# The last two output tiles of an attention-plus-MLP kernel: another copy out of PSUM and another cut of the store

## The chip, the cores and the metric

One core of one Trainium2 chip. The metric is device time of the whole program in microseconds, as the median of several executions of the compiled kernel; lower is better.

## What is computed

Attention with a position bias, batch 4, 8 heads, 576 positions, head dimension 64, and behind it a two-layer MLP with a squared ReLU on the 4 x 576 = 2304 token rows of 512 numbers. All inputs and the output are float32.

```python
def _attn_ref(q, k, v, w1, b1, w2):
    ...
    attn = np.exp(scores)
    attn = attn / (np.sum(attn, axis=-1, keepdims=True) + 1e-09)
    return np.matmul(attn, v).astype(np.float32)

def _moe_ref(x, w_in, w_out):
    h = x @ w_in
    r = np.maximum(h, 0.0)
    g = r * r
    return (g @ w_out).astype(np.float32)
```

`x` is the attention's output as a matrix of 2304 x 512, `w_in` is 512 x 2048, `w_out` 2048 x 512. Rows 576 b to 576 b + 575 of the result belong to batch b.

## The kernel before, in words

The program runs in two stages. The attention stage fills the first half of the span; the MLP stage is a hand-written order of work (`tc.manual_schedule()`, so the order of the code is the order on each engine). The change lies at the very end of the MLP stage.

The MLP stage walks over `items`, pairs of a token group `n` and a slice `P` of the hidden width. Groups 0 to 3 are the first 512 positions of each batch. The fifth group, `n == B`, holds the rest: the last 64 positions of each of the four batches, 256 rows in all, packed as two tiles of 128 rows. Tile k = 0 has the tails of batches 0 and 1, tile k = 1 those of batches 2 and 3, 64 partitions for each batch. This group comes last, and its last item is the last of the program.

For an item, `products` (line 1192) makes the hidden activations on TensorE, `sums`, `squares` and `parts_g` turn them into the operands `gh` and `gl` of the second layer, and `down` (line 1284) adds their products with `w_out` into PSUM banks `y`, one bank of 128 x 512 for each tile of 128 rows. For the very last item `down` sorts its matmuls by tile, so that tile 0 is complete before the matmuls of tile 1 begin. After the last matmul of a tile `down` calls `leave`, which copies the bank from PSUM into a fresh SBUF tile `o` and sends it to DRAM.

For groups 0 to 3 the store is line 1267: 512 KB, two tiles at a time, 128 partitions outermost. For the group of tails `leave` takes another path (lines 1246 to 1251): VectorE copies the right half of the bank (line 1247), ScalarE the left half (line 1248), and SyncE issues one transfer of 256 KB (line 1250). Its DRAM side is a view of `out` with the batch outermost: 2 batches x 64 rows x 512.

All transfers of the kernel before are issued by SyncE, on its one queue. ScalarE issues none. At the end (line 1403) SyncE waits for the transfers that are still under way, and then the engines meet and the program ends.

Of the kernel before, what the change touches and what calls it, by code (L numbers as in the profile page):

```python
# [21 lines left out]
B, H, S, D = 4, 8, 576, 64  # L22
# [55 lines left out]
def attention_then_relu2_mlp(ctx: ExitStack, tc: tile.TileContext, q, k, v, cols, w_in, w_out, psi, xmat, dist, out):  # L78
    nc = tc.nc
    PE, DVE, ACT, POOL, SP = nc.tensor, nc.vector, nc.scalar, nc.gpsimd, nc.sync  # L80
# [1151 lines left out]
    def pair_tile():  # L1232
        return stage_p["p"].tile([128, 2, 512], F32, name="o", tag="stage", bufs=2)
# [8 lines left out]
    def leave(n, P, k):  # L1242
        y = y_t[n][k]
        j, x = divmod(k, 2)
        if n == B:
            o = ready_y[j] = pair_tile()
            DVE.tensor_copy(out=o[:, 0, 256:], in_=y[:, 256:])
            ACT.copy(o[:, 0, :256], y[:, :256])
            tails = out.rearrange("(b s) m -> b s m", s=S)[2 * k:2 * k + 2, 512:]
            SP.dma_start(out=tails, in_=o[:, 0])  # L1250
            return
        if (n, 0) in part_y:
            o = ready_y[j]
            DVE.tensor_tensor(out=o[:, x], in0=o[:, x], in1=y, op=ALU.add)
        else:
            if x == 0:
                ready_y[j] = pair_tile()
            o = ready_y[j]
            ACT.copy(o[:, x], y)
        if x == 0:  # L1260
            return
        if P < NP - 1:
            ready_y[j, "dram"] = dram.tile([128, 1024], F32, name=f"py{j}")
            SP.dma_start(out=ready_y[j, "dram"], in_=o.rearrange("p x m -> p (x m)"))
        else:
            rows = out[S * n + 256 * j:S * n + 256 * j + 256].rearrange("(x p) m -> p x m", x=2)
            SP.dma_start(out=rows, in_=o)

    def down(i):
        n, P = items[i]  # L1270
        w = width[n]
        nk = w // 64
        if (n, P) in firsts:
            banks = {k: py_p.tile([128, 512], F32, name=f"y{k}") for k in (2, 3, 0, 1) if k < nk}
            y_t[n] = [banks[k] for k in range(nk)]
        order = [(f, k, m) for f in range(2) for ms in ((0, 1), (2,)) for k in range(nk) for m in ms]
        if i == NI - 1:
            order.sort(key=lambda x: x[1])
        for f, k, m in order:
            wh, wl = w_t[4 * P + 2 + f]  # L1280
            gh, gl = g_t[i, f]
            t, o = divmod(128 * k, w)
            slot = t if f else 1 - t
            PE.matmul(  # L1284
                y_t[n][k], lhsT=(gl if m == 2 else gh)[:, slot, o:o + 128], rhs=wl if m == 1 else wh,
                start=((n, P) in firsts and f == 0 and m == 0), stop=((n, P) in lasts and f == 1 and m == 2),
            )
            if (n, P) in lasts and f == 1 and m == 2:
                leave(n, P, k)
        if (n, P) in lasts and P < NP - 1:  # L1290
            for j in range(2):
                part_y[n, j] = ready_y[j, "dram"]

    tmp_p = tmp_stack.enter_context(tc.tile_pool(name="tmp", bufs=1, side="right", reuse_waits="tile"))
    with tc.manual_schedule():
# [3 lines left out]
        for i in range(NI + 1):  # L1299
# [49 lines left out]
            if i < NI and (n, P) in firsts:  # L1349
                r = run_of[n, P]  # L1350
# [56 lines left out]
```

## Time and profile before

| What | Value |
|---|---|
| Time, median of 3 runs | 713.63 us (713.4 to 714.18) |
| Span of the profiled execution, first to last instruction | 712.7 us |
| Own time of the profiled execution | not listed beside the span; the median of the runs is 0.93 us above the span |
| TensorE busy | 685.8 us, 96% of the span |
| VectorE busy | 552.1 us, 77% |
| ScalarE busy | 472.8 us, 66% |
| GpSimd busy | 196.7 us, 28% |
| DMA, mean over the span | 105 GB/s |

The profile is of one execution on the one core. Busy time is a mean over the whole span; the last stretch has to be read by itself, in views limited to a window of time. In those, SPq stands for an instruction of SyncE that issues a transfer: its duration is that of the issue, not of the transfer. The share of the DMA is the mean busy share of the core's 16 DMA engines, and packets are what these engines moved: one per row of 2 KB here, and a small one with which each participating engine reports that it is done.

### The profile page before, as it was taken

The numbers are of one execution on the slowest core, as the hardware profiler recorded it, in microseconds if no ns is written. First come the engines' busy times: TensorE is split into PE (matmuls) and PEld (weight loads), VectorE is DVE, ScalarE is ACT, GpSimd is POOL, SyncE is SP. The second block draws the span as 40 slices with busy tenths as digits, with TensorE's granted clock in tenths as the row PEclk, the third lists the DMA queues.
The fourth block names the chain that finished last, engine by engine and source line by source line (L and its number), as shares of the span: only waits on it lengthen the run. The fifth ranks groups of instructions, "written<-read, shape, count | busy, mean of one in ns | idle before, by whom it ended". The sixth has DMA issues, their size and how long they took to land.

```text
span 712.7 us, 17402 instructions
## 1 busy us (share of the span) xinstructions
PE 685.8 (96%) x6966; PEld 568.7 (80%) x6966; DVE 552.1 (77%) x1165; ACT 472.8 (66%) x954; POOL 196.7 (28%) x313
## 2 busy tenths in 40 slices
PE   7899999999999999999999999999999999999992
PEld 6678888887787877778788888888888888888881
DVE  7999888876688998998888868687567964566761
ACT  5678878878777999997666757765475554464220
POOL 5464544442111344653223113121111220000000
PEclk9999999999999999999999999999999999999997
DMA  6740000007476234111901433230076403433100
GB/s 190 209 118 3 19 2 3 2 19 219 171 246 205 55 94 128 65 31 56 359 1 61 184 127 119 86 136 1 1 246 256 149 22 142 176 105 119 60 2 29
DMA packets 31620, 75.13 MB, mean 105 GB/s; under 512 B 5556, under 2 KB 13876, under 8 KB 30516
## 3 DMA queue, kind: packets, MB, share of 16 engines
q1 hardware_dynamic: 31540, 74.03, 31.1%
q8 instruction: 55, 0.90, 0.5%
q14 instruction: 25, 0.20, 0.1%
HBM read 55.66 MB, written 18.35 MB: 104 GB/s over the span
## 4 chain that ended last, share of the span: by engine, by line
PE 86%; DVE 7%; ACT 2%; issue 1%; POOL 1%; DMA 0%; SPq 0%; ACTq 0%; POOLq 0%; DVEq 0%
PE y L1284 28%; PE ha L1192 13%; PE sp L425 11%; PE px L547 10%; PE hb L1192 9%; PE pp L529 8%; PE bb L383 5%; DVE t L438 2%; DVE mask L373 1%; ACT pt L1123 1%; PE pa L521 1%; ACT p L445 1%; DVE bt L391 1%; DMA area<-in_psi 0%; DVE xT L496 0%
## 5 line engine op out<-in xcount | busy, mean ns | idle before, releaser
L1192 PEld LDWEIGHTS <-area 128*128 128x128 f16 x1680 | 147.7, 98 | 25.3 <-issue 8.4
L1284 PE MATMUL y<-w,gh 128*128 128x512 f32 x576 | 149.0, 398 | 0.6 <-ACT gh L1228 0.6
L1284 PEld LDWEIGHTS y<-w,gh 128*128 128x128 f32 x576 | 105.1, 188 | 22.2 <-ACT gh L1228 1.3
L438 DVE CUSTOM_DVE_ANT_0 t<-sp,area 128x576 f32<-128x576 f32 x144 | 104.2, 753 | 22.4 <-PE sp L425 12.0
L445 ACT ACTIVATE p<-t,negm 128x576 f32<-128x576 f32 x144 | 113.0, 795 | 2.7 <-DVE negm L438 2.1
L425 PE MATMUL sp<-k,q 64*128 64x288 f32 (+1 forms) x640 | 98.9, 426 | 5.5 <-DVE negm L438 4.0
L547 PE MATMUL px<-pt,v 128*64 128x128 f32 (+1 forms) x1600 | 92.2, 266 | 0.0
L547 PEld LDWEIGHTS px<-pt,v 128*64 128x64 f32 x1600 | 79.2, 137 | 11.5 <-ACT pt L1123 6.4
L1192 PE MATMUL ha<-area 128*128 128x256 f16 (+1 forms) x816 | 85.1, 260 | 0.7 <-DVE c L1209 0.7
L399 POOL TENSOR_TENSOR area<-bt,bt 128x256 f32<-128x256 f32 x72 | 66.0, 921 | 69.1 <-DVE bt L391 67.5
L1284 PE MATMUL y<-w,gl 128*128 128x512 f32 x288 | 79.0, 390 | 0.0
L529 PE MATMUL pp<-ident,p 128*128 128x128 f32 x576 | 78.1, 278 | 0.0
L529 PEld LDWEIGHTS pp<-ident,p 128*128 128x128 f32 x576 | 62.6, 141 | 17.7 <-ACT p L445 7.2
L425 PEld LDWEIGHTS sp<-k,q 64*128 64x128 f32 (+1 forms) x640 | 52.9, 175 | 25.4 <-issue 6.1
L1192 PE MATMUL hb<-area 128*128 128x256 f16 (+1 forms) x612 | 64.7, 260 | 0.0
L1284 PEld LDWEIGHTS y<-w,gl 128*128 128x128 f32 x288 | 54.1, 188 | 12.2 <-DVE gl L1229 0.2
L373 DVE TENSOR_TENSOR mask<-sdist,theta 128x1024 f16<-128x1024 f16 x81 | 57.9, 720 | 2.5 <-PE bb L383 0.5
L851 ACT COPY pt<-pp 128x512 f32<-128x512 f32 x68 | 36.9, 589 | 32.2 <-PE pp L529 32.2
L383 PE MATMUL bb<-wmov,mask 128*128 128x64 f16 x1296 | 46.9, 197 | 4.2 <-DVE mask L373 4.1
L1123 ACT COPY pt<-pp 128x512 f32<-128x512 f32 x76 | 41.4, 602 | 13.5 <-PE pp L529 13.1
L383 PEld LDWEIGHTS <-mask 128*128 128x128 f16 x1296 | 44.9, 101 | 6.5 <-DVE mask L373 5.9
L1229 DVE TENSOR_TENSOR gl<-area,gh 128x512 fp32r<-128x512 f32 (+1 forms) x40 | 25.3, 668 | 27.3 <-ACT gh L1228 25.5
(161 smaller groups left out, 992.8 us busy)
## 6 DMA issues: line engine op xcount, KB each, us to landing
raw<-in_w_in SPq DMA_DIRECT2D x32, 512.0 KB, 4.4
r<-in_w_out SPq DMA_DIRECT2D x16, 512.0 KB, 5.3
xs<-area SPq DMA_DIRECT2D x4, 1792.0 KB, 12.7
py<-o SPq DMA_DIRECT2D x12, 512.0 KB, 2.7
o<-py SPq DMA_DIRECT2D x12, 512.0 KB, 4.5
v<-in_v SPq DMA_DIRECT2D x16, 320.0 KB, 3.9
q<-in_q SPq DMA_DIRECT2D x32, 128.0 KB, 3.5
out<-o SPq DMA_DIRECT2D x8, 512.0 KB, 2.9
```

What stands on the lines that cost most here:

```text
L373: DVE.tensor_tensor(out=out, in0=win, in1=th, op=ALU.is_ge)
L383: PE.matmul(bb[:, 64 * (7 - r):64 * (8 - r)], lhsT=m[:, r], rhs=wmov[:, n], start=(n == 0), stop=(n == 1))
L399: POOL.tensor_tensor(out=dst, in0=tw, in1=sw, op=ALU.add)
L425: mm = PE.matmul(out_t[to, x, :HALF], lhsT=qt[rows, cols], rhs=kt[rows, k0:k0 + HALF], start=True, stop=True)
L438: DVE.tensor_tensor_reduce(out=t.rearrange("p (x n) -> p x n", x=2), in0=sp[:, :, :HALF], in1=bias.rearrange("p (x n) -> p x n", x=2), sca ...
L445: ACT.activation(out=p[:, S * n:S * n + S], in_=t, func=AF.Exp, bias=negm[:, n:n + 1], scale=-1.0, accum_out=sums[:, 2 * ic + n:2 * ic + n ...
L529: PE.transpose(pp[:, 128 * c:128 * c + 128], p[:, k0:k0 + 128], ident)
L547: PE.matmul(px[64 * h:64 * h + 64, 128 * m:128 * m + w], lhsT=vt[:, c, h], rhs=src, start=(c == 0), stop=(c == 4))
L851: ACT.copy(dst, src)
L1123: ACT.copy(*c)
L1192: PE.matmul(h[:, s, :w], lhsT=a, rhs=x, start=(k == 0), stop=(k == 5))
L1284: PE.matmul(y_t[n][k], lhsT=(gl if m == 2 else gh)[:, slot, o:o + 128], rhs=wl if m == 1 else wh, start=((n, P) in firsts and f == 0 and m ...
```

## The change

The last two tiles leave PSUM in one VectorE copy each, 128 x 512, and ScalarE copies nothing there. Each tile then goes to DRAM as two transfers, one for each batch: 64 partitions of `o` to 64 consecutive rows of `out`, 128 KB, so that the rows are the outermost dimension on both sides. SyncE issues the first of the two, ScalarE the second.

```diff
         if n == B:
             o = ready_y[j] = pair_tile()
-            DVE.tensor_copy(out=o[:, 0, 256:], in_=y[:, 256:])
-            ACT.copy(o[:, 0, :256], y[:, :256])
-            tails = out.rearrange("(b s) m -> b s m", s=S)[2 * k:2 * k + 2, 512:]
-            SP.dma_start(out=tails, in_=o[:, 0])
+            DVE.tensor_copy(out=o[:, 0], in_=y)
+            for r, queue in enumerate((SP, ACT)):
+                end = S * (2 * k + r + 1)
+                queue.dma_start(out=out[end - 64:end], in_=o[64 * r:64 * r + 64, 0])
             return
```

On ScalarE the end of the program changes as follows (`gh` are the operands of the last matmuls, `y_9466` and `y_9467` the PSUM banks of tiles 0 and 1):

```order
 L1206 ACTIVATE area<-ha,small 128x4x128
 L1228 CAST gh<-area 128x2x128 x2
-L1248 COPY o<-y_9466 128x256
-L1248 COPY o<-y_9467 128x256
+L1250 DMA out<-o 64x512 x2
 L1403 UNCONDITIONAL_BRANCH
```

The two copies are gone and two issues of transfers stand in their place, the first that this engine makes.

On SyncE, whose last rows are loads of partial sums, the stores of a full group and then those of the tails:

```order
 L1240 DMA o<-py_8025 128x1024
 L1267 DMA out<-o 128x2x512 x2
-L1250 DMA out<-o 2x64x512 x2
+L1250 DMA out<-o 64x512 x2
 L1403 UNCONDITIONAL_BRANCH
```

There are still two issues here, each for half as many bytes and without the outer dimension of two. VectorE keeps its two copies at their places, twice as wide. TensorE and GpSimd have the same rows as before.

## Rows read from the trace of the kernel before

**Rows 1.** The page's chain of work that ended last, share of the span by engine.
```profile
PE 86%; DVE 7%; ACT 2%; issue 1%; POOL 1%; DMA 0%; SPq 0%; ACTq 0%; POOLq 0%; DVEq 0%
```

**Rows 2.** Timeline from 697 us: start, duration, engine, line, operation, idle before it.
```profile
697.72 0.42 DVE L1247 COPY o<-y 128x256 f32<-128x256 f32 x1 [0.96 <-PE y L1284]
...
698.57 1.92 SPq L1250 DMA_DIRECT2D out<-o  x2
698.67 0.39 PE L1284 MATMUL y<-w,gl 128*128 128x512 f32 x1
699.10 0.42 DVE L1247 COPY o<-y 128x256 f32<-128x256 f32 x1 [0.96 <-PE y L1284]
699.56 0.37 ACT L1248 COPY o<-y 128x256 f32<-128x256 f32 x1 [1.01 <-DVE o L1247]
```

**Rows 3.** SyncE's waits from 660 us: us in total, times, longest.
```profile
SPq L1403 <- DMA out<-o: 11.1, 2, 6.0
```

**Rows 4.** Stretches of the end: busy us by engine, granted clock, DMA share, GB/s.
```profile
699.80:700.00 0.20, 0.00 (x0) 0.00 (x0) 0.00 (x0) 0.13 (x1) 0.00 (x0) 1.00 0.14 41
700.00:711.20 11.20, 0.00 (x0) 0.00 (x0) 0.00 (x0) 0.00 (x0) 0.00 (x0) 0.62 0.13 46
711.20:711.40 0.20, 0.00 (x0) 0.00 (x0) 0.00 (x0) 0.00 (x0) 0.00 (x0) 0.50 0.06 21
711.40:712.70 1.30, 0.00 (x0) 0.00 (x0) 0.00 (x0) 0.00 (x0) 0.00 (x0) 0.50 0.00 0
```

**Rows 5.** DMA packets from 690 to 713 us.
```profile
DMA packets 261, 0.54 MB, mean 24 GB/s; under 512 B 4, under 2 KB 4, under 8 KB 260
```

**Rows 6.** Lines 1250 and 1267: issue duration in ns, first and last start; landing.
```profile
L1250 SPq DMA_DIRECT2D out<-o x2: 542/609/676, 698.6 to 700.0; - x2
...
L1267 SPq DMA_DIRECT2D out<-o x8: 383/389/398, 601.9 to 661.6; - x8
...
DMA to landing us min/median/max: 2.8/2.9/3.0
```

**Rows 7.** Timeline of SyncE's issues: the program's first, and the last two of line 1267.
```profile
0.72 0.41 SPq L122 DMA_DIRECT2D area<-in_cols  x1
...
660.38 1.58 SPq L1267 DMA_DIRECT2D out<-o  x2
```

**Rows 8.** Stretches around the last two stores of line 1267.
```profile
661.20:661.40 0.20, 0.20 (x7) 0.20 (x5) 0.20 (x1) 0.20 (x1) 0.00 (x0) 1.00 0.57 215
661.40:664.00 2.60, 2.60 (x21) 2.23 (x19) 2.53 (x8) 0.39 (x1) 0.00 (x0) 1.00 1.01 379
664.00:664.20 0.20, 0.20 (x2) 0.15 (x2) 0.20 (x1) 0.00 (x0) 0.00 (x0) 1.00 0.31 103
```

**Rows 9.** DMA packets from 661 to 666 us.
```profile
DMA packets 544, 1.05 MB, mean 210 GB/s; under 512 B 32, under 2 KB 32, under 8 KB 544
```

**Rows 10.** A stretch near the start, in which loads of 64 partitions run.
```profile
5.20:5.90 0.70, 0.70 (x6) 0.70 (x5) 0.63 (x6) 0.68 (x2) 0.00 (x0) 1.00 0.82 236
```

**Rows 11.** DMA issues: tile, count, KB each, median us from issue to landing.
```profile
k<-in_k SPq DMA_DIRECT2D x16, 144.0 KB, 3.7
...
area<-in_cols SPq DMA_DIRECT2D x1, 37.0 KB, 1.9
```

**Rows 12.** The tile k: issues of line 157, duration in ns min/median/max.
```profile
L157 SPq DMA_DIRECT2D k<-in_k x16: 465/595/597, 4.0 to 278.9; - x16
```

**Rows 13.** VectorE groups by shape: count, busy us, mean ns of one, idle before.
```profile
L1254 DVE TENSOR_TENSOR o<-o,y 128x512 f32<-128x512 f32 x24 | 14.9, 682 | 10.0 <-PE y L1284 10.0
...
L560 DVE COPY xT<-px 128x128 f32<-128x128 f32 x36 | 10.2, 284 | 5.8 <-PE px L547 5.8
...
L560 DVE COPY xT<-px 128x256 f32<-128x256 f32 x12 | 5.0, 415 | 0.0
...
L1247 DVE COPY o<-y 128x256 f32<-128x256 f32 x2 | 0.8, 425 | 1.9 <-PE y L1284 1.9
```

**Rows 14.** ScalarE groups: the longest item on it at the program's start.
```profile
L319 ACT ACT_TABLE_LOAD x1 | 1.3, 1283 | 0.7 <-PEq L1397 0.7
```

## The prediction, made before the result was known

> **What bounds the kernel now.** The page's chain of waits gives TensorE 86% and the DMA nothing [rows 1], which reads as if stores could not matter. But that chain ends with the last instruction that an engine executes, and a transfer is none. So read the end of the timeline next [rows 2]. The last matmul of tile 1 starts at 698.67 and takes 0.39, so TensorE is done at 699.06. VectorE's half copy runs from 699.10 to 699.52, ScalarE's from 699.56 to 699.93, one after the other. Then no engine computes any more, and the span has 712.7 - 699.9 = 12.8 us to go.
>
> What fills them stands in the stretches of the end [rows 4]. The DMA engines begin after 699.8 and stop between 711.2 and 711.4, at a share of 0.13 and 46 GB/s. A share of 0.13 is 2 of 16 engines (0.125). The packets say it a second time: among those of the two stores 4 are small ones [rows 5], two per store, so each store ran on two engines; two stores of line 1267 leave 32 [rows 9], sixteen each. Line 1250 has 2 as its outermost dimension, line 1267 has 128. SyncE issues both tail stores back to back (1.92 us from 698.57, so to 700.49 [rows 2]) and then waits 11.1 us for them [rows 3]: to 711.6. From there 712.7 - 711.6 = 1.1 us of closing instructions follow.
>
> So the end is set by 512 KB that leave through two engines. Whatever shortens that comes off the time one for one, until the next thing in the tail is late.
>
> **The change, part by part.**
>
> *The copies.* One VectorE copy of 128 x 512 replaces 0.42 + 0.04 + 0.37 = 0.83 us of VectorE and ScalarE in turn. The trace has no such copy. From PSUM, 128 columns take 284 ns and 256 take 415 [rows 13], 1.02 ns a column; adding 256 columns to the 425 ns of line 1247 gives 687. Line 1254, which reads the same bank at full width, takes 682. I take 0.685. Tile 1 is then in SBUF at 699.10 + 0.685 = 699.79 where it was at 699.93: a gain of 0.15. Tile 0 is ready at 697.72 + 0.685 = 698.41, well before VectorE's next copy at 699.10, so it delays nothing; nobody is queued behind either copy. ScalarE loses two copies that nothing else waited for.
>
> *The issues.* SyncE and ScalarE issue at 699.80, side by side. A store of line 1267 takes SyncE 389 ns to issue, one of line 1250 609 [rows 6], loads of 64 rows up to 597 [rows 12]. The first data moved 1.3 us after the first issue of line 1250 (698.57 to 699.8 or later), and 0.9 us after the pair of line 1267 (660.38 [rows 7], first data after 661.2 [rows 8]). I take 1.0: nearer to line 1267, which is also a store on 16 engines, and 0.1 more for the longer issue of 64 rows. What tile 0's two transfers move is through by then: issued at 698.42, 8 rows an engine.
>
> *The data.* That 64 rows outermost spread over many engines is shown near the start, where the loads of 64 partitions (lines 136, 156 and 157) keep 0.82 of the 16 engines busy [rows 10], not 0.13. At full spread the stores of line 1267 move 379 GB/s with 1.01 of the engines [rows 8]: a row of 2 KB then takes one engine 16 x 2048 / 379 = 86 ns. Tile 1 has 128 rows, 8 an engine if its two transfers share the same 16: 0.69 us. Had each queue engines of its own, it would be 4 rows and 0.35. No row shows a second queue at work, since SyncE issues everything. I take the shared case.
>
> The Trainium skill, on the page "DMA: Bandwidth & Descriptors", section "Issuing engines are not separate DMA queues", says the same: transfers of several issuers run on the same 16 DMA engines, and a second issuer saves only the time to initiate. Its "Rules for kernel authors" go further and advise against cutting a tile into two transfers of half the partitions. By these two places the second queue brings only an issue; with engines of its own for each queue the sum would come out 0.35 lower, at 703.55.
>
> *The landing.* The last packets of line 1267 end after 664.0, and its second issue, at 660.38 + 1.58 - 0.39 = 661.57, has landed 3.0 us later at the most [rows 6], at 664.6: 0.4 to 0.5 us behind them. I take 0.4.
>
> From issue to landing that is 1.0 + 0.69 + 0.4 = 2.09 us. Bounds: not under 1.5 (0.82 + 0.35 + 0.35, everything at its best), and not over 3.7, the median landing of the 64-row loads of k [rows 11], which queue behind other loads as these stores don't.
>
> The Trainium skill prices one transfer on the GpSimd path at about 2.0 us fixed plus bytes over 436 GB/s (same page, "Anatomy of one DMA"). By that figure, an estimate for 256 KB would be 2.6 us and the sum 0.5 higher, at 704.4; no run here has a transfer on that path.
>
> *The closing.* The 1.1 us from the landing to the last instruction stay. Two more completions are waited for, both long in or arriving together: nothing.
>
> *The rest* of the program has the same instructions at the same places on every engine: nothing, both ways.
>
> **The sum.** 699.80 + 2.09 = 701.89 for the landing, against 711.6; 9.7 us less. The span goes from 712.7 to 703.0. The median of the runs stands 0.93 above the profiled span, for launch and end outside it; carried over, **703.9 us**, 1.4% faster. With the bounds for the landing, 703.3 to 705.5.
>
> **The rivals.**
>
> *Not spread after all.* If the four transfers still went through two engines, 128 rows each at 46 GB/s would again take 11.4 us; only the copy and a shorter issue would be won, some 0.4 us: 713.2. For it: a store of 64 partitions does not occur in the trace, only loads. Against it: rows 10, and the count of small packets, which follows the outermost dimension in both stores that the trace has.
>
> *A cold or slow second queue.* ScalarE has issued nothing before. Its first issue comes at 698.42, 1.38 us before the one that counts, so a first-time cost of up to about 0.8 us is hidden (its own issue takes 0.6). Beyond that the second follows late, and SyncE waits for it. For it: nothing in the trace prices ScalarE's first issue, and the first things on ScalarE are 1.28 us table loads [rows 14], the longest of its items for the program's own upkeep; at that price the end moves by some 0.5, at 2 to 3 us by 1 to 2. Against it: SyncE's own first issue, at the very start, took 0.41 us and landed in 1.9 [rows 7, 11]. Time: 704.4 to 706.
>
> *Slower: the same mechanism at another size.* If ScalarE's part of tile 1 lands later than 711.6, the old landing, the change loses. It decides at a first-time cost of 711.6 - 698.42 - 0.6 - 1.8 = 10.8 us for ScalarE's issue (or as much spent outside the span on setting up a second queue at each launch, where 0.93 is all there is now). At 13 us it would be about 715.8. Nothing in the trace that is waited for at its first use is near that size: 1.28 us is the largest on ScalarE. The whole gain hangs on two transfers of an engine that never issued one, though, so it gets a little.
>
> **How the numbers follow.** My forecast gets 85%, a dear second queue or a partial spread 10%, no spread 2%, slower 3%. A measurement of this kernel can tell some 0.2%, 1.4 us, from no change. Forecast and second case are faster by more than that (95%), no spread is the same (2%). The range: down to 702.9, the lower bound less 0.4 for the spread between runs (the median of before has 0.2 and 0.55 to its sides), up to 705.8, which takes in the upper bound and most of the second case.
>
> **What would show it.** Right: in the stretch behind the last matmul the DMA share is near 0.9 or more for under a microsecond, not 0.13; four stores leave 64 small packets; VectorE's copies take about 0.69 us; SyncE's wait for the stores falls from 11.1 to about 1.5 us; the span ends near 3.9 us after the last matmul (699.06 to 703.0). Wrong: a share that stays near 0.13 (no spread), a long gap between ScalarE's first issue and its data (second queue), or a later last matmul, which would mean that the change reached the work before the tail.

## The result, and the profile after

| | Before | After |
|---|---|---|
| Time, median | 713.79 us (713.40 to 714.18, 4 runs) | 704.49 us (704.21 to 705.03, 4 runs) |
| Ratio after to before, 95% interval | | 0.9869 [0.9858, 0.9881] |
| Span of the profiled execution | 712.7 us | 702.8 us |
| Last matmul ends | 699.06 | 698.47 |
| From there to the end of the span (before rounding) | 13.63 us | 4.37 us |

9.3 us less, 1.3%. The third and fourth rows are the ones to compare: the end of the last matmul moved by half a microsecond between the two profiled executions of the changed kernel (below), the stretch behind it by less than 0.1. That stretch shrank by 13.63 - 4.37 = 9.3 us, so the whole difference lies there. In the experiments the profiled execution of the run with the old cut on two queues was a disturbed one (span 1170.6 us); of it only the DMA rows are read.

The timeline of the end, after, in the columns of [rows 2]:

```profile
697.86 1.85 SPq L1250 DMA_DIRECT2D out<-o  x2
697.87 1.87 ACTq L1250 DMA_DIRECT2D out<-o  x2
698.08 0.39 PE L1284 MATMUL y<-w,gl 128*128 128x512 f32 x1
698.50 0.69 DVE L1247 COPY o<-y 128x512 f32<-128x512 f32 x1 [0.67 <-PE y L1284]
```

The issues of line 1250 (duration in ns, minimum, median and maximum):

```profile
L1250 SPq DMA_DIRECT2D out<-o x2: 488/508/529, 697.9 to 699.2; - x2
L1250 ACTq DMA_DIRECT2D out<-o x2: 510/538/565, 697.9 to 699.2; - x2
```

The half copy of ScalarE is gone, VectorE's copy takes 0.69, and both engines issue at once behind each copy: the second pair leaves at 699.2 (697.86 + 1.85 less the 0.49 of an issue).

The stretches behind it, columns as in [rows 4]:

```profile
698.60:699.00 0.40, 0.00 (x0) 0.00 (x0) 0.40 (x1) 0.00 (x0) 0.00 (x0) 1.00 0.00 0
699.00:700.20 1.20, 0.00 (x0) 0.00 (x0) 0.19 (x1) 0.00 (x0) 0.00 (x0) 1.00 0.82 219
700.20:700.40 0.20, 0.00 (x0) 0.00 (x0) 0.00 (x0) 0.00 (x0) 0.00 (x0) 1.00 0.26 61
700.40:701.00 0.60, 0.00 (x0) 0.00 (x0) 0.00 (x0) 0.00 (x0) 0.00 (x0) 1.00 0.93 191
701.00:701.40 0.40, 0.00 (x0) 0.00 (x0) 0.00 (x0) 0.00 (x0) 0.00 (x0) 1.00 0.91 333
701.40:702.80 1.40, 0.00 (x0) 0.00 (x0) 0.00 (x0) 0.00 (x0) 0.00 (x0) 0.79 0.01 1
```

Two bursts of about 1.1 us, one for each tile, at a share near 0.9 where before there were 11.4 us at 0.13 [rows 4]. Read the last two columns (DMA share and GB/s) of the fourth and fifth row together: the engines are as busy in both, but move 191 GB/s in the one and 333 in the other. Share x 16 engines x 2048 bytes / rate is the time that a row of 2 KB takes an engine: 0.93 x 16 x 2048 / 191 = 160 ns, then 90. That difference was not in my sum.

The DMA packets and queues of the end, after, against [rows 5]:

```profile
DMA packets 321, 0.54 MB, mean 39 GB/s; under 512 B 64, under 2 KB 64, under 8 KB 320
## 3 DMA queue, kind: packets, MB, share of 16 engines
q1 hardware_dynamic: 160, 0.26, 9.1%
q10 hardware_dynamic: 160, 0.26, 4.9%
...
out<-o SPq DMA_DIRECT2D x2, 128.0 KB, 2.4
out<-o ACTq DMA_DIRECT2D x2, 128.0 KB, 2.7
```

64 small packets for four stores are sixteen engines each, where [rows 5] had two each. SyncE's queue (q1) and ScalarE's (q10) carry the same bytes, but q1's packets took nearly twice the engines' time: the slow rows are SyncE's, the fast ones ScalarE's. ScalarE's stores, issued at the same moment, land 0.3 us later.

The kernel before has the same two speeds, with one queue and two engines:

```profile
699.80:702.00 2.20, 0.00 (x0) 0.00 (x0) 0.00 (x0) 0.13 (x1) 0.00 (x0) 1.00 0.14 30
703.00:711.00 8.00, 0.00 (x0) 0.00 (x0) 0.00 (x0) 0.00 (x0) 0.00 (x0) 0.50 0.13 51
```

Its first rows took 0.14 x 16 x 2048 / 30 = 153 ns each, the later ones, tile 1's among them, 84. The 46 GB/s of [rows 4] is the mean of the two.

SyncE's wait for the stores, against [rows 3]:

```profile
SPq L1403 <- DMA out<-o: 2.0, 2, 1.2
```

### The profile page after: what moved, and what is told of

Same layout as the page of the kernel before. It is cut to its first block, busy times and chain, and to the rows that moved or that the text cites. A ratio compares the mean times of both kernels' runs of the same rounds, so it can differ in the third digit from the quotient of the medians.

```text
span 702.8 us, 17399 instructions
## 1 busy us (share of the span) xinstructions
PE 685.8 (98%) x6966; PEld 568.7 (81%) x6966; DVE 552.5 (79%) x1165; ACT 471.8 (67%) x952; POOL 196.4 (28%) x313
## 4 chain that ended last, share of the span: by engine, by line
PE 87%; DVE 8%; ACT 2%; issue 1%; POOL 1%; DMA 0%; ACTq 0%; POOLq 0%; DVEq 0%
PE y L1284 28%; PE ha L1192 13%; PE sp L425 11%; PE px L547 11%; PE hb L1192 10%; PE pp L529 8%; PE bb L383 5%; DVE t L438 2%; DVE mask L373 1%; ACT pt L1123 1%; PE pa L521 1%; ACT p L445 1%; DVE bt L391 1%; DVE xT L496 0%; PE ra L490 0%
## 5 line engine op out<-in xcount | busy, mean ns | idle before, releaser
L1123 ACT COPY pt<-pp 128x512 f32<-128x512 f32 x76 | 41.4, 602 | 13.5 <-PE pp L529 13.3
```

The costliest lines, as they stand in the source:

```text
L1123: ACT.copy(*c)
```

## The experiments

All are the changed kernel with one edit. The measure to compare is the stretch from the end of the last matmul to the end of the span, called the tail here; the time tells only what exceeds about 0.2%.

**The changed kernel again.** No edit.

> The changed kernel once more, beside the next three on the same chip. Theory (sixteen engines instead of two carry the tail's 512 KB): 704.2 to 705.0 us, 9.3 less than before. Second reading, on the time outside the span: the changed kernel's runs lie 1.75 to 1.83 us above their spans, the kernel before 0.93 by median against one span; if that is the price of a second queue, the runs of before on this chip stay near 0.9 above their spans and this one near 1.8. If it is only which run was profiled, both show the same.

Measured: 705.03 us (704.15 to 705.3), ratio 0.9876 [0.9861, 0.9891]. The profiled execution took 704.15 with a span of 702.4; its last matmul ended at 697.99 (start 697.60, 0.39 long), so the tail is 4.4 again. The 19 runs of before on that chip have a median of 713.95, and their spans, 712.2 in the middle one, lie 1.8 below. Both kernels spend 1.8 us outside the span: a second queue costs nothing there. The 0.93 that I had read came from setting the span of one execution beside the median of others.

**All stores on SyncE.**

```diff
-            for r, queue in enumerate((SP, ACT)):
+            for r, queue in enumerate((SP, SP)):
```

> All four 64-row stores issued by SyncE, none by ScalarE. Theory A (the spread over the engines is the whole gain, the second queue saves an issue): SyncE issues tile 1's second store some 0.5 us after the first, its data follow the first's, and the span ends 0 to 0.4 us later than the changed kernel's, 702.6 to 703.3. If the second queue costs 0.9 us outside the span, the time is then lower by 0.5 to 0.9 than the changed kernel's (703.6 to 704.2); if it costs nothing, 704.5 to 705.0. Theory B (the second queue brings bandwidth of its own): the data take twice as long, 705.3 or more.

Measured: 704.3 us (704.26 to 704.88), ratio 0.987 [0.9854, 0.9887], not to be told from the change. Last matmul, and the burst for tile 1:

```profile
697.58 0.39 PE L1284 MATMUL y<-w,gl 128*128 128x512 f32 x1
```
```profile
699.80:701.20 1.40, 0.00 (x0) 0.00 (x0) 0.00 (x0) 0.00 (x0) 0.00 (x0) 0.59 0.86 192
701.20:702.50 1.30, 0.00 (x0) 0.00 (x0) 0.00 (x0) 0.00 (x0) 0.00 (x0) 0.50 0.00 0
```
```profile
DMA to landing us min/median/max: 2.3/2.3/2.4
```

The tail is 702.5 - 697.97 = 4.5 to 4.6. The second queue is worth 0.1 to 0.2 us of the 9.3; theory B falls. All rows now take about 0.86 x 16 x 2048 / 192 = 147 ns, those of a tile's second store too, though it follows right behind the first. All four stores land within 2.3 to 2.4 us of their issue, so the second was not held up.

**Two queues, the old cut.**

```diff
-                end = S * (2 * k + r + 1)
-                queue.dma_start(out=out[end - 64:end], in_=o[64 * r:64 * r + 64, 0])
+                half = slice(256 * r, 256 * r + 256)
+                queue.dma_start(out=tails[:, :, half], in_=o[:, 0, half])
```

(`tails` as in the kernel before, batch outermost.)

> The one copy and the two queues of the change, but each store keeps the batch outermost (2 x 64 rows x 256 columns). Theory A (two engines per store, the same two for both queues): the tail stays near 11.5 us of data, DMA share 0.13, 713 to 714.5. Theory B (each queue has engines of its own): four engines at work, share 0.25, data in half the time, 707.5 to 709.

Measured: 714.7 us, ratio to before 1.0009 [0.9999, 1.0019]. The gain is gone with the cut, although two queues work. Packets and queues of the end, then a stretch of it:

```profile
DMA packets 521, 0.54 MB, mean 17 GB/s; under 512 B 8, under 2 KB 520, under 8 KB 520
```
```profile
1162.00:1169.00 7.00, 0.00 (x0) 0.00 (x0) 0.00 (x0) 0.00 (x0) 0.00 (x0) 0.50 0.14 48
```

8 small packets for four stores, two engines each, and a share of 0.14 instead of 0.25: both queues use the same two. This is the run that separates the second queue from the cut, and it is all the cut.

**62 rows instead of 64.**

```diff
-                queue.dma_start(out=out[end - 64:end], in_=o[64 * r:64 * r + 64, 0])
+                for lo, hi in ((0, 62), (62, 64)):
+                    queue.dma_start(out=out[end - 64 + lo:end - 64 + hi], in_=o[64 * r + lo:64 * r + hi, 0])
```

> Rows outermost and two queues as in the change, but each batch's 64 rows go as 62 and 2, eight stores in all. Theory A1 (the number of engines is the largest number up to 16 that divides the outermost count; 62 gives 2): the stores of 62 rows run on two engines, the share is 0.13 and the small packets are few (2 per store), 711 to 714. Theory A2 (rows outermost are dealt out to all sixteen, four or so each, whatever the count): share near 0.9, and four more issues cost 0.5 to 1: 704.8 to 705.8.

Measured: 713.89 us, ratio to before 0.9999 [0.999, 1.0009]: the rows are outermost and the whole gain is gone.

```profile
DMA packets 273, 0.54 MB, mean 23 GB/s; under 512 B 16, under 2 KB 16, under 8 KB 272
```
```profile
700.00:709.00 9.00, 0.00 (x0) 0.00 (x0) 0.00 (x0) 0.00 (x0) 0.00 (x0) 0.50 0.13 47
```

16 small packets for eight stores, two engines each. So "rows outermost" is not what counts; the number of rows does. The Trainium skill has the rule, on the page "DMA: Bandwidth & Descriptors" in the section "Why a DMA increments its semaphore by 16 and not by 1": a transfer runs on the largest number of engines up to 16 that divides the outermost sizes of both its sides. The small packets agree with it in each cut of this case: 2 batches gave 2, 64 rows 16, 62 rows (2 x 31) 2.

**All stores on ScalarE.**

```diff
-            for r, queue in enumerate((SP, ACT)):
+            for r, queue in enumerate((ACT, ACT)):
```

> All four 64-row stores issued by ScalarE. In the change SyncE's rows of 2 KB take an engine some 160 ns each and ScalarE's, which start when SyncE's are through, 84; with SyncE alone all take 155. Theory G (a store of 64 partitions is fed to the engines no faster than a row per engine in 155 ns as it starts; one that waits behind another has been prepared meanwhile and runs at 84): ScalarE alone gives 155 ns too, its store 1.15 us after issue at the first row, last landing as with SyncE alone, span 702.3 to 703.3, time 704.2 to 705. Theory Q (ScalarE's queue is the faster one): rows at 84, the last landing 0.5 to 0.6 us earlier than with SyncE alone, time 703.6 to 704.2.

Measured: 704.46 us (703.78 to 705.01), ratio 0.9867 [0.9852, 0.9882]. A stretch of the burst for tile 1:

```profile
699.40:700.60 1.20, 0.00 (x0) 0.00 (x0) 0.00 (x0) 0.00 (x0) 0.00 (x0) 0.87 0.91 200
```

0.91 x 16 x 2048 / 200 = 149 ns a row, as with SyncE alone. ScalarE's queue is not the faster one; theory Q falls. The slow second-queue rival of the prediction falls with it: four stores on ScalarE cost no more than four on SyncE.

**One store of 128 partitions for a tile.** The tails of two batches are interleaved row by row in the tile, so that a store has 64 rows outermost in DRAM and 128 partitions in SBUF.

```diff
-        return [(slice(64 * r, 64 * r + 64), xT[r][:, :, 512:], tail_x(2 + r)) for r in range(2)]
+        return [(slice(r, 128, 2), xT[r][:, :, 512:], tail_x(2 + r)) for r in range(2)]
...
-            for r, queue in enumerate((SP, ACT)):
-                end = S * (2 * k + r + 1)
-                queue.dma_start(out=out[end - 64:end], in_=o[64 * r:64 * r + 64, 0])
+            tails = out.rearrange("(b s) m -> b s m", s=S)[2 * k:2 * k + 2, 512:]
+            SP.dma_start(out=tails.rearrange("b s m -> s b m"), in_=o[:, 0])
```

> The tails of two batches interleaved row by row in a tile (the operands of the last token group are written with a step of 2), so that a tile goes to DRAM as one store of 128 partitions with 64 rows outermost on the DRAM side, issued by SyncE alone. Theory A (engines are all that counts): sixteen engines, 32 small packets in all, same as the change within 0.6 us. Theory G adds: 128 partitions run at 86 ns a row as line 1267 does, so 0.7 us of data, landing 2.0 to 2.2 us after the issue instead of 2.64 of the last store of the change, span 0.4 to 0.6 us shorter behind the last matmul (3.8 to 4.0 instead of 4.4); time 703.6 to 704.4. If the rows cost 155 ns here as well: no gain behind the last matmul, 4.3 to 4.6.

Measured: 704.17 us (703.87 to 704.47), ratio 0.9862 [0.9846, 0.9878].

```profile
697.81 1.95 SPq L1249 DMA_DIRECT2D out<-o  x2
698.04 0.39 PE L1283 MATMUL y<-w,gl 128*128 128x512 f32 x1
```
```profile
out<-o SPq DMA_DIRECT2D x2, 256.0 KB, 2.4
```
```profile
700.40:701.20 0.80, 0.00 (x0) 0.00 (x0) 0.00 (x0) 0.00 (x0) 0.00 (x0) 1.00 0.87 328
```

Rows at 0.87 x 16 x 2048 / 328 = 87 ns, as line 1267 has them [rows 8]. The tail is 702.6 - 698.43 = 4.2, only 0.2 shorter than the change's and above the 3.8 to 4.0 expected: the row time came out as theory G had it, but the first data moved only some 1.2 us behind the issue at 699.2, where I had counted on about 1.0.

**The half copies with the new stores,** and **the single copy with the old store.** Each keeps one part of the change:

```diff
-            DVE.tensor_copy(out=o[:, 0], in_=y)
+            DVE.tensor_copy(out=o[:, 0, 256:], in_=y[:, 256:])
+            ACT.copy(o[:, 0, :256], y[:, :256])
```

> The stores of the change with the two half copies of before (VectorE, then ScalarE). My sum gave the single copy 0.15 us: from the last matmul to tile 1's issues 0.87 to 0.90 us here and 0.74 with the single copy; time 704.4 to 705.3, not to be told from the change. If the copies were worth more (or the half copies overlap), 0.3 us or more either way in that stretch.

```diff
-            for r, queue in enumerate((SP, ACT)):
-                end = S * (2 * k + r + 1)
-                queue.dma_start(out=out[end - 64:end], in_=o[64 * r:64 * r + 64, 0])
+            tails = out.rearrange("(b s) m -> b s m", s=S)[2 * k:2 * k + 2, 512:]
+            SP.dma_start(out=tails, in_=o[:, 0])
```

> The single copy of the change with the stores of before (2 x 64 rows, SyncE alone). Nothing but 0.15 us should be won: two engines, share 0.13, 4 small packets, 11.4 us of data, 713.4 to 714.4. If the single copy were what unlocked the tail, 705.

Measured: the new stores alone 704.81 us, ratio 0.9872 [0.9852, 0.9892], tail 703.0 - 698.53 = 4.5; the single copy alone 713.82, ratio 0.9998 [0.9987, 1.0008], tail 712.6 - 699.06 = 13.5. So of the 9.3 us the copy brings 0.1, the stores the rest. The last matmul of each, and SyncE's wait in the second run, back where [rows 3] had it:

```profile
698.14 0.39 PE L1285 MATMUL y<-w,gl 128*128 128x512 f32 x1
```
```profile
698.67 0.39 PE L1283 MATMUL y<-w,gl 128*128 128x512 f32 x1
```
```profile
SPq L1402 <- DMA out<-o: 11.1, 2, 6.0
```

**The stores of tile 0 held back,** to see whether a store that has waited runs faster. The code issued them behind tile 1's copy; its edit is that of the next run with `range(2)` in place of `(1, 0)`.

> The stores of the change, but those of tile 0 wait until tile 1 is copied: SyncE then issues two 64-row stores in a row, ScalarE two. Theory G (a 64-partition store runs at some 155 ns a row when the engines are ready for it as it starts, at 84 when it has waited): of the four stores only the first to run, SyncE's first, shows about 155; ScalarE's first and SyncE's second, which wait behind it, run at 84 to 100. If instead SyncE's stores are slow by themselves whenever ScalarE issues beside it, SyncE's second shows 155 to 160 as well. Behind the last matmul 4.7 to 5.3 us instead of 4.4; time 704.8 to 705.8.

Measured: 704.39 us, tail 4.4 where 4.7 to 5.3 were expected, the same two bursts as in the change. It did not test what it was meant to: on its queue a store waits only for its own tile's copy, and nothing ahead of it held it, so the stores of tile 0 left early as before. The next run puts tile 1's stores ahead of them on both queues:

```diff
+            c_t["o", k] = o
+            if k == 0:
+                return
-            for r, queue in enumerate((SP, ACT)):
-                end = S * (2 * k + r + 1)
-                queue.dma_start(out=out[end - 64:end], in_=o[64 * r:64 * r + 64, 0])
+            for kk in (1, 0):
+                for r, queue in enumerate((SP, ACT)):
+                    end = S * (2 * kk + r + 1)
+                    queue.dma_start(out=out[end - 64:end], in_=c_t["o", kk][64 * r:64 * r + 64, 0])
```

> As the run before the last was meant: SyncE and ScalarE each issue tile 1's store first and tile 0's behind it, so that all four leave behind the last copy. Theory G: SyncE's first store shows about 155 to 160 ns a row, ScalarE's first, which waits behind it, 84; SyncE's second, issued 0.5 us after its first and held up behind both, has waited some 0.5 us when the engines come free and shows less than 155, 84 to 110; ScalarE's second 84. If SyncE's stores are slow whenever ScalarE issues beside it: 155 to 160 for SyncE's second too. Behind the last matmul 4.9 to 5.3 us by G, 5.3 to 5.6 by the other; time 704.9 to 706.

Measured: 705.18 us, tail 703.4 - 698.02 = 5.4: above the 4.9 to 5.3 that G gave, and inside the 5.3 to 5.6 of the other theory. The tail alone would speak against G, so the rows have to decide.

```profile
698.77 1.18 SPq L1254 DMA_DIRECT2D out<-o  x2
698.78 1.45 ACTq L1254 DMA_DIRECT2D out<-o  x2
```
```profile
700.00:700.60 0.60, 0.00 (x0) 0.00 (x0) 0.00 (x0) 0.00 (x0) 0.00 (x0) 1.00 0.93 191
700.60:701.00 0.40, 0.00 (x0) 0.00 (x0) 0.00 (x0) 0.00 (x0) 0.00 (x0) 1.00 0.98 359
701.00:701.40 0.40, 0.00 (x0) 0.00 (x0) 0.00 (x0) 0.00 (x0) 0.00 (x0) 1.00 0.95 343
701.40:702.00 0.60, 0.00 (x0) 0.00 (x0) 0.00 (x0) 0.00 (x0) 0.00 (x0) 1.00 0.61 191
```
```profile
q1 hardware_dynamic: 160, 0.26, 7.1%
```

One store of 128 KB lasts 0.69 us at 191 GB/s, from just before 700.0 to about 700.7. The next 0.8 us move (359 + 343) x 0.4 = 281 KB at some 90 ns a row: two stores, ScalarE's first and SyncE's second. That SyncE's second is among them shows in its queue (q1): its packets took 7.1% of 14 us of the 16 engines, in the change 9.1%. That is 0.02 x 16 x 14 us = 4.5 us less, 70 ns for each of the 64 rows of one store. So a store of SyncE does run fast when it has waited behind others, beside a busy ScalarE, as G had it. G was wrong on ScalarE's second store: the last stretch gives 0.61 x 16 x 2048 / 191 = 105 ns a row instead of 84, and the tail came out longer. That a store is prepared while it waits is my reading of it; the runs show the speed, not the preparing.

**Two half copies, a store behind each.** The interleaved tails of the one-store version; ScalarE's half goes to a free tile.

```diff
-            DVE.tensor_copy(out=o[:, 0], in_=y)
+            oh = xT[3][:, k, :256]
+            DVE.tensor_copy(out=o[:, 0, 256:], in_=y[:, 256:])
+            ACT.copy(oh, y[:, :256])
...
+            tails = out.rearrange("(b s) m -> b s m", s=S)[2 * k:2 * k + 2, 512:].rearrange("b s m -> s b m")
+            SP.dma_start(out=tails[:, :, 256:], in_=o[:, 0, 256:])
+            ACT.dma_start(out=tails[:, :, :256], in_=oh)
```

> The interleaved tails of the one-store version, with two half copies into two tiles and a store of 128 partitions x 256 columns behind each: VectorE's half by SyncE, ScalarE's half by ScalarE. ScalarE's copy still stands behind VectorE's. SyncE's store leaves 0.48 us after the last matmul and ScalarE's 0.89, rows of 1 KB at about 46 ns; if the landing is set by issue to first data (1.15) plus ScalarE's own 0.4 us of data, the end comes 0.2 to 0.4 us earlier than with one store: 3.8 to 4.0 us behind the last matmul instead of 4.2. If a second issuer delays (its data 1.8 us after the issue, as in the change), no gain: 4.3 to 4.6. Time 703.6 to 704.6 either way, not to be told from one store.

Measured: 704.14 us (703.65 to 704.45), ratio 0.9863 [0.9846, 0.9881].

```profile
698.37 0.39 PE L1286 MATMUL y<-w,gl 128*128 128x512 f32 x1
698.80 0.42 DVE L1248 COPY o<-y 128x256 f32<-128x256 f32 x1 [0.95 <-PE y L1286]
699.25 0.37 ACT L1249 COPY xT<-y 128x256 f32<-128x256 f32 x1 [1.00 <-DVE o L1248]
699.66 0.55 ACTq L1252 DMA_DIRECT2D out<-xT  x1
```

The tail is 702.7 - 698.76 = 3.9, the shortest of all and 0.5 less than the change's, as expected. By the tail, in one execution, it beats both kernels; by its time it can't be told from the change, since 0.5 us is under the 0.2% that the times resolve.

## Why the prediction was right, step by step

The forecast was 703.9 and the time is 704.49, inside the range; 9.7 us less was expected, 9.3 came, by the mechanism named.

- **The end is set by stores on two engines:** right, and now shown from both sides. With the cut undone (two queues, old cut) or with a count of rows that gives two engines (62), the time is that of before to 0.1%; with 64 rows on either queue, or 64 x 2 rows in one store, it is 704 to 705.
- **The copy, 0.15 us:** right. It takes 0.69 against the 0.685 taken, and by itself it shortens the tail by 0.1.
- **Issue to first data, 1.0 us:** too low by some 0.15. SyncE issued at 699.2 and its data moved from just under 700.4.
- **The data, 0.69 us at 86 ns a row:** the term that was mis-sized. The row on which it stood [rows 8] is a store of 128 partitions. SyncE's stores of 64 partitions took 160 ns a row, ScalarE's behind them 90, and the burst about 1.1 us: 0.4 more. The trace of before held two hints: [rows 10], read like [rows 8], gives 0.82 x 16 x 2048 / 236 = 114 ns for 2 KB of loads into 64 partitions (with rows of other lengths), and the first rows of the old stores took 153.
- **The landing, 0.4 us, and the closing, 1.1:** 0.3 to 0.4 measured, and about 1.0. Here the sum was some 0.15 too high, which offsets the issue, so that the 0.4 of the data is what is left: a tail of 4.4 instead of 3.9, and a wait of SyncE of 2.0 us instead of 1.5.
- **The second queue shares the engines:** right. It brings 0.1 to 0.2 us; with SyncE alone the burst lasts 1.4 us instead of 1.1. The Trainium skill ("DMA: Bandwidth & Descriptors", "Rules for kernel authors") advised against two transfers of half the partitions; the one-store run agrees, by 0.2 us.
- The Trainium skill's fixed 2.0 us plus bytes over 436 GB/s ("DMA: Bandwidth & Descriptors", "Anatomy of one DMA", for the GpSimd path) gave an estimate of 2.6 us and 704.4, which the median meets. That is in part luck. The change's last landing came 2.6 to 2.7 us behind its issue, but in other parts (1.15 us to the first data, 1.1 of data, 0.4 to the landing), and the case that the estimate prices, one transfer of 256 KB, took 2.4 in the one-store run, on SyncE's queue.
- **The rivals:** no spread happened only in the kernels built to have it, and then gave 713.8 to 714.7 where I had said 713.2. The dear second queue did not show: ScalarE's two issues took 0.51 and 0.57 us, so no first-time cost shows, ScalarE alone gives 704.46, and the time outside the span is 1.8 us in all kernels. In the sum for the slower rival, the 1.8 us behind the issue has no row; with the 2.09 of the forecast its turning point is 10.5 us instead of 10.8. My 0.93 was a slip, two executions set beside each other; it dropped out of the difference.

## What to carry to other kernels

When no engine computes any more and the span goes on, look at the DMA share of that stretch before anything else: here 0.13 was two of sixteen engines, and the small packets per transfer counted them. A transfer's outermost size, not its bytes or its number of queues, decided how many engines carried it here: 64 gave sixteen, 2 and 62 gave two. The chain of waits does not show such a tail, since it ends with the last instruction.

## What the runs showed that was not expected

A store of 64 partitions that was not held up took 147 to 160 ns for a row of 2 KB and engine, on either queue, at a share of 0.9, even right behind another of its own queue (SyncE alone, ScalarE alone). The stores that had to wait behind the other queue's took about 90: ScalarE's in the change, and with tile 1 first ScalarE's first and SyncE's second (ScalarE's second took 105). A second queue is not needed for the higher speed: in the kernel before, on one queue, the rows went from 153 ns to 84 as the store ran on. Nor does the number of partitions alone decide it: the stores of before have 128 and started slow, those of the one-store run have 128 and took 87. Why some start slow stays open. The work ahead of the tail, the same in nearly all of these kernels, ended between 697.4 (ScalarE alone) and 699.1 us (before) in their profiled executions, while the tail of the changed kernel was 4.4 in both of its own. Single times scatter by some 1 us; in these two executions none of it lies in the tail.
